# A three-layer kernel on one core: one subtraction moved to GpSimd, layer 2 one slice later, both heads' states in one instruction, contiguous weight slices

## The chip, the cores and the metric

The program runs on one core of one Trainium2 chip. Its engines are TensorE (PE in the profile; its weight loads have a row of their own, PEld), VectorE (DVE), ScalarE (ACT), GpSimd (POOL) and SyncE (SP, which issues DMAs). Each engine works off its own list of instructions in order and waits on semaphores for the others. The metric is the device time of one execution in microseconds (us), the median of several; lower is better.

## The reference

Three layers follow one another. Only the arithmetic that matters here is kept:

```python
# 1: recurrence over S=768 tokens for B=4, H=8, D=48; state is D x D per batch and head
for t in range(S):
    cur   = einsum('bhd,bhe->bhde', u*k[t], v[t])
    y[t]  = einsum('bhd,bhde->bhe', r[t], state + cur)
    state = w[t][..., None]*state + einsum('bhd,bhe->bhde', k[t], v[t])
x = y as (3072 tokens, 384)
# 2: dense layer, w_in 384 x 2048, w_out 2048 x 384
h = maximum(x @ w_in, 0);  x = (h*h) @ w_out
# 3: 8 experts, top 1, tokens with x @ w_skip <= 0 pass unchanged
e = argmax(x @ w_gate);  g = softmax(x @ w_gate)[e]
out = x + g * (maximum(x @ w1[e], 0) @ w2[e])
```

The inputs may come as 64-bit floats; the kernel reads them as words and makes 32-bit floats of the weights itself.

## The kernel before, in words

**Tiling.** The 3072 tokens are cut into 12 units of 256 tokens (`UT`). Stage A computes layer 1 of a unit, stage B layer 2 with the routing scores as ten more output columns, stage C the experts. A and B run as one pipeline: while B works on unit i, A works on a later unit. Stage C begins when all units are through B.

**Precision.** Each float32 operand of layers 2 and 3 is split into two parts, a rounded one (`h` in the names: `xth`, `wih`, `woh`, `gh`) and the rest (`l`: `xtl`, `wil`, `wol`, `gl`), and three products are added. The rest is always made by subtracting the rounded part from the whole.

**Stage B.** One unit has 16 slices of 128 hidden columns. `b_l1` of a slice is nine matmuls of 256 columns into one of two PSUM banks `ph`. ScalarE makes `g` from it by relu and square (L346, L347) and rounds it to `gh` (L348); VectorE subtracts (L349):

```python
        nc.scalar.copy(gh, g)
        nc.vector.tensor_tensor(gl, g, gh.bitcast(F32), ALU.subtract)
```

`b_l2` of the slice is six matmuls of 394 columns (L357) that add to the two PSUM banks `acc`; the third and the sixth read `gl`. There are two sets of `g`, `gh`, `gl`, used in turn. `route` then copies `acc` out (L369, L370), writes the unit's rows and computes each token's place in the lists of the experts, with small VectorE instructions (L385 to L441) and two indirect DMAs from GpSimd (L446).

**Stage A.** A half unit `H` has two head pairs, and `elem(H)` does its elementwise work: two scans on VectorE (L190, L205), products on GpSimd (L198 and L229 `ru`, L210 `bsc`, L241 `kbd`, L235 `gr`), a scaling on ScalarE (L228). From unit 3 on VectorE transposes `kbd` into `knd` (L216). The tensor work of head pair `P` is `pair_steps(P)` with six steps: `s1p` (L265) and `s1v` (masked copies, L275) make the products within chunks of 64 tokens; `s2p` (L286) makes each chunk's addition to the state in `pu`; `s2v` carries the state from chunk to chunk; `s3p` (L310) applies it; `s3v` splits the result into B's operand. In `s2v` each chunk and each of the two heads of a pair has an instruction of its own, of 48 partitions, on VectorE (L300 for a sequence's first chunk, else L302), and the state is written straight into `vz`, where `s3p` reads it:

```python
                for h in range(2):
                    sl = slice(64 - 64 * h, 112 - 64 * h)
                    u_ps = pu[sl, c * 48:(c + 1) * 48]
```

**Weights of B.** For each of 16 slices `w_load` fetches 128 columns of `w_in` and 128 rows of `w_out` by two DMAs from SP, `w_dec` turns words into float32 on VectorE (L509 to L511, tile `stf`), `w_split` rounds on ScalarE (L518, L521) and subtracts on GpSimd or, where the table `lw` has a 1, on VectorE (8 of 32; L520, L522). `w9_tp` to `w9_f` make the ten score columns. `raw` and `stf` have two buffers each. `consts` fills small tables on VectorE (L473 to L478).

**Order.** Every piece of work is put into one list of events with a time in slices of B: `b_l1` of slice g has the time g + 0.09, `b_l2` of slice g the time g + 1.256, and the pieces of A have times from the tables `PRM` (the first units) and `STP` (all later ones). The list is sorted by time and written out; this sets the order on every engine. Nothing is reordered at run time.

Of the kernel before, what the change touches and what calls it, by code (L numbers as in the profile page):

```python
# [84 lines left out]
def rwkv_moe_kernel(ctx: ExitStack, tc: tile.TileContext, a_in, v_in, ud, w_in, w_out,  # L85
# [170 lines left out]
    def pair_steps(P):  # L256
# [56 lines left out]
        def s3v():  # L313
# [3 lines left out]
            if P < 8 and PRM["ly"][P]:  # L317
                yf = bp.tile([128, 2, DM], F32, tag="x2", name="x2", bufs=1)[:, 0, 0:UT]
                nc.scalar.copy(yf, y)
                nc.scalar.copy(hi, yf)  # L320
                nc.gpsimd.tensor_tensor(lo, yf, hi.bitcast(F32), ALU.subtract)
            else:
                nc.scalar.copy(hi, y)
                nc.vector.tensor_tensor(lo, y, hi.bitcast(F32), ALU.subtract)
# [164 lines left out]
    dec, wot = {}, {}  # L489

    def w_load(j):
        s = slice(j * 128, (j + 1) * 128)
        if w_in.dtype == F32:
# [1 line left out]
            nc.sync.dma_start(f[:, 0].rearrange("p (k n) -> p k n", k=KC),
                              w_in[:, s].rearrange("(k p) f -> p k f", p=128))
            nc.sync.dma_start(f[:, 1], w_out[s])
# [550 lines left out]
```

## Time and profile before

| | us |
|---|---|
| median of 3 runs | 980.1 (976.5 to 981.46) |
| span of the profiled execution, first to last instruction | 978.3 |
| VectorE busy | 690.6 |
| TensorE busy | 832.3 |
| GpSimd busy | 413.5 |
| ScalarE busy | 410.0 |

The profiled execution has no time of its own beside its span; the median of the runs stands 1.8 us above that span. The program has five stretches. From 0 to 94 us the first unit of A runs and the first weights are decoded. From 94 to 159 B's first unit runs beside the rest of the weights. From 159 to 641 A and B run together, one unit after another. At 641 a branch on the range of the decays ends the pipeline of A, and B's last unit runs beside the loading of expert weights. From 690 to 978 the experts run. TensorE's busy time is modelled for pipelined matmuls, so the waits of PEld show its stalls best.

### The profile page before, as it was taken

To read this page: it belongs to the slowest core of one execution; us is meant where nothing else is said; L and a number is where in the kernel's file an instruction comes from. 1 tells how busy PE (TensorE), PEld (TensorE's weight loads), DVE (VectorE), ACT (ScalarE), POOL (GpSimd) and SP (SyncE) were. 2 spreads that over 40 slices of the span, in tenths; PEclk is the share of its full clock that TensorE was granted. 3 is DMA by queue.
4 is the path that set the end of the run, shared out by engine and by line. 5 is a ranking of instruction groups with operands and counts; after the bars stand their busy time and mean duration, and the time that the engine had idled before them with its cause. 6 is when DMAs were issued, how large, how long until landed. Compare 5 with 4: busy or idle time off the path is not lost. (4 is left out here: it accounts for less than half of the span.)

```text
span 978.3 us, 17865 instructions
## 1 busy us (share of the span) xinstructions
PE 832.3 (85%) x6528; PEld 772.1 (79%) x6528; DVE 690.6 (71%) x1605; ACT 410.0 (42%) x1020; POOL 413.5 (42%) x409
## 2 busy tenths in 40 slices
PE   2666899999899999899999899989899779787844
PEld 2555799989788888788888788989899779776743
DVE  7997977788888888888888888535633266256631
ACT  1233556545454545454545454457222123123410
POOL 7754635443434343434343434002822256254540
PEclk9999799999999999999999999989999899898877
DMA  8435212231313131313131311055621155153510
GB/s 199 142 127 173 98 44 77 65 80 41 84 37 86 38 90 30 88 33 88 37 99 21 93 27 51 9 167 176 194 66 33 45 173 171 41 180 119 195 32 6
DMA packets 75625, 86.93 MB, mean 89 GB/s; under 512 B 32020, under 2 KB 68008, under 8 KB 75456
## 3 DMA queue, kind: packets, MB, share of 16 engines
q1 hardware_dynamic: 68080, 72.53, 26.2%
q0 software_dynamic: 4736, 11.18, 3.5%
q10 hardware_dynamic: 2640, 1.23, 0.6%
q8 instruction: 74, 1.21, 0.5%
q14 instruction: 95, 0.78, 0.3%
HBM read 68.44 MB, written 15.16 MB: 85 GB/s over the span
## 5 line engine op out<-in xcount | busy, mean ns | idle before, releaser
L342 PE MATMUL ph<-xt,wih 128*128 128x256 f32 x1152 | 226.9, 293 | 3.4 <-PEq L709 3.4
L342 PEld LDWEIGHTS ph<-xt,wih 128*128 128x128 f32 x1152 | 185.0, 192 | 6.7 <-issue 3.7
L342 PE MATMUL ph<-xt,wil 128*128 128x256 f32 x576 | 164.1, 285 | 0.0
L357 PE MATMUL acc<-woh,gl 128*128 128x394 f32 x384 | 136.7, 356 | 29.3 <-DVE gl L349 29.3
L349 DVE TENSOR_TENSOR gl<-g,gh 128x256 fp32r<-128x256 f32 x192 | 98.3, 512 | 78.4 <-ACT gh L348 77.4
L346 ACT ACTIVATE g<-ph 128x256 f32<-128x256 f32 x192 | 73.9, 385 | 183.1 <-PE ph L342 171.3
L357 PE MATMUL acc<-woh,gh 128*128 128x394 f32 x384 | 134.0, 349 | 0.6 <-ACT gh L348 0.6
L357 PE MATMUL acc<-wol,gh 128*128 128x394 f32 x384 | 131.6, 343 | 0.0
L342 PEld LDWEIGHTS ph<-xt,wil 128*128 128x128 f32 x576 | 110.8, 192 | 0.0
L357 PEld LDWEIGHTS acc<-woh,gl 128*128 128x128 f32 x384 | 72.8, 189 | 44.1 <-DVE gl L349 43.6
L229 POOL TENSOR_TENSOR ru<-ain,fsc 112x512 f32<-112x512 f32 x23 | 28.2, 1228 | 180.3 <-ACT ain L228 180.2
L816 DVE SCALAR_TENSOR_TENSOR gl<-ph,gh 128x256 fp32r<-128x256 f32 x80 | 33.6, 422 | 89.0 <-ACT gh L815 88.8
L302 DVE SCALAR_TENSOR_TENSOR vz<-vz,wsw,pu 48x48 f32<-48x48 f32 x320 | 84.3, 263 | 10.3
L275 DVE COPY_PREDICATED gr<-cis,pat 64x256 f32<-64x256 int32 x192 | 85.1, 443 | 8.9 <-PE pat L265 4.6
L815 ACT ACTIVATE gh<-ph 128x256 fp32r<-128x256 f32 x80 | 30.7, 384 | 135.3 <-PE ph L812 135.3
L347 ACT ACTIVATE g<-g 128x256 f32<-128x256 f32 x192 | 80.2, 418 | 6.1
L348 ACT CAST gh<-g 128x256 fp32r<-128x256 f32 x192 | 77.9, 406 | 6.1
L357 PEld LDWEIGHTS acc<-woh,gh 128*128 128x128 f32 x384 | 73.4, 191 | 1.9 <-ACT gh L348 1.2
L357 PEld LDWEIGHTS acc<-wol,gh 128*128 128x128 f32 x384 | 73.4, 191 | 0.0
L772 POOL DMA_INDIRECT out<-yo,lsb x22 | 22.0, 1001 | 113.4 <-DVE yo L771 70.4
L265 PE MATMUL pat<-ru,kbd 112*128 112x128 f32 x384 | 56.5, 295 | 15.4 <-POOL kbd L241 14.5
L265 PEld LDWEIGHTS pat<-ru,kbd 112*128 112x128 f32 x384 | 53.9, 209 | 15.6 <-POOL kbd L241 14.5
(187 smaller groups left out, 1799.3 us busy)
## 6 DMA issues: line engine op xcount, KB each, us to landing
raw<-in_w SPq DMA_DIRECT2D x64, 384.0 KB, 4.1
ain<-in_a_in SPq DMA_DIRECT2D x23, 675.9 KB, 5.2
raw<-in_w_in SPq DMA_DIRECT2D x16, 384.0 KB, 3.9
raw<-in_w_out SPq DMA_DIRECT2D x16, 384.0 KB, 4.5
vz<-in_v_in SPq DMA_DIRECT2D x44, 128.0 KB, 5.2
x2d<-x SPq DMA_DIRECT2D x12, 384.0 KB, 2.5
out<-x SPq DMA_DIRECT2D x12, 384.0 KB, 3.1
xt<-yt SPq DMA_DIRECT2D x72, 32.0 KB, 2.0
```

The source lines that it names most:

```text
L229: nc.gpsimd.tensor_tensor(st["ru"][:, :, :, 1, :], r, st["f"][:, :, :, 1:65], ALU.mult)
L265: nc.tensor.matmul(pat[:, c], kb[0:112, qq, c, :], ru[:, qq, c], start=True, stop=True)
L275: nc.vector.copy_predicated(gr[sl, qq, :, h, :], msk[sl].unsqueeze(1).to_broadcast([64, 4, CH]), pat[sl, :, m, :])
L302: nc.vector.scalar_tensor_tensor(zn, hv[H][sl, qq, c, h, 0:48], wsw[sl, q, b, cg:cg + 1], u_ps, ALU.mult, ALU.add)
L342: nc.tensor.matmul(h[:, 0:UT], w[:, kc, j * 128:(j + 1) * 128], x[:, kc, :], start=(n == 0), stop=(n == 3 * KC - 1))
L346: nc.scalar.activation(g, h[:, 0:UT], AF.Relu)
L347: nc.scalar.activation(g, g, AF.Square)
L348: nc.scalar.copy(gh, g)
L349: nc.vector.tensor_tensor(gl, g, gh.bitcast(F32), ALU.subtract)
L357: nc.tensor.matmul(acc[t][:, 0:OW], a[:, s], w[:, j, :], start=(j == 0 and n == 0), stop=(j == NJ - 1 and n == 2))
L815: nc.scalar.activation(hhs[f % 2], h[:, 0:UT], AF.Relu)
L816: nc.vector.scalar_tensor_tensor(hls[f % 2], h[:, 0:UT], 0.0, hhs[f % 2].bitcast(F32), ALU.max, ALU.subtract)
```

## The change

- **gl on GpSimd.** In `b_l1` the subtraction that makes `gl` is issued on GpSimd instead of VectorE. `gh` and `gl` get three buffers (`NPB`) that slices take in turn; `g` keeps two.
- **Layer 2 later.** `b_l2` of slice g has the time g + 2.256 instead of g + 1.256, except at the ends of the last two units; `route` of units 0 to 9 is one slice later too.
- **States.** `s2v` makes one instruction of 112 partitions for a chunk of both heads, into new tiles `zt` and `zcs`. A new step `s2c` copies the states from there into `vz` on ScalarE: two copies for a pair, four for the second pair of a half unit unless it ends a sequence.
- **Weights.** The host lays `w_in` and `w_out` out as one array `wio`, so that a slice is one contiguous DMA. All 32 subtractions of `w_split` are on GpSimd.
- **First steps.** `consts` moves from time -16.5 to 9. The small copies `o_w` and the scaling `o_us` have times of their own; in steady state `o_w` is 0.9 slices later and `o_us` 0.9 slices earlier. The pool of the decode buffers closes at time 7 instead of 27.3. Some tiles live in other pools.

```diff
 STP = {
-    "b": [0.09, 1.256],
+    "b": [0.09, 2.256],
 PRM = {
-    "c": -16.511,
+    "c": 9,
...
+        def o_us():
+            r, k, w = hin[H]
+            if H >= 4 or PRM["lu"][H]:
+                for q in range(2):
+                    nc.scalar.activation(r[:, q], r[:, q], AF.Copy, scale=uds[:, q0 + q:q0 + q + 1])
...
         def s2v():
+            zt, zc = zts[P % 2], zcs[:, q]
             for c in range(4):
                 cg = 4 * th + c
                 if cg == 11:
                     continue
-                for h in range(2):
-                    sl = slice(64 - 64 * h, 112 - 64 * h)
-                    u_ps = pu[sl, c * 48:(c + 1) * 48]
-                    zn = (hv[H][sl, qq, c + 1] if c < 3 else vzs[(H + 2) % 3][sl, qq, 0])[:, h, 0:48]
...
+                u_ps = pu[0:112, c * 48:(c + 1) * 48]
+                zn = zt[:, c] if c < 3 else zc
+                if cg == 0:
+                    nc.vector.tensor_copy(zn, u_ps)
+                else:
+                    nc.vector.scalar_tensor_tensor(zn, zt[:, c - 1] if c else zc, wsw[:, q, b, cg:cg + 1], u_ps,
+                                                   ALU.mult, ALU.add)
+
+        def s2c():
+            zt = zts[P % 2]
+            for h in range(2):
+                sl = slice(64 - 64 * h, 112 - 64 * h)
+                nc.scalar.copy(hv[H][sl, qq, 1:4, h, 0:48], zt[sl])
+                if qq and th < 2:
+                    nc.scalar.copy(vzs[(H + 2) % 3][sl, :, 0, h, 0:48], zcs[sl, q - 1:q + 1])
...
-        g, gh, gl = pgs[j % 2]
+        g = pgg[j % 2]
+        gh, gl = pgs[(NJ * i + j) % NPB]
...
-        nc.vector.tensor_tensor(gl, g, gh.bitcast(F32), ALU.subtract)
+        nc.gpsimd.tensor_tensor(gl, g, gh.bitcast(F32), ALU.subtract)
...
-        sv = w_in.bitcast(I32)[:, 2 * j * 128:2 * (j + 1) * 128].rearrange("(k p) f -> p k f", p=128)
-        nc.sync.dma_start(raw[:, 0].rearrange("p (k n) -> p k n", k=KC), sv)
-        nc.sync.dma_start(raw[:, 1], w_out.bitcast(I32)[s])
+        nc.sync.dma_start(raw.rearrange("p a b -> p (a b)"), wio.bitcast(I32)[j])
...
-        lo = [nc.vector if PRM["lw"][2 * j + n] else nc.gpsimd for n in range(2)]
-        lo[0].tensor_tensor(wil[:, :, s], fi, wih[:, :, s].bitcast(F32), ALU.subtract)
+        nc.gpsimd.tensor_tensor(wil[:, :, s], fi, wih[:, :, s].bitcast(F32), ALU.subtract)
...
-            atv(16 * (i + 1) + (STP["r"][n] if n or i < NU - 2 else 0.01), f)
+            atv(16 * (i + 1) + (1 + STP["r"][n] if i < NU - 2 else STP["r"][n] if n else 0.01), f)
...
-        atv(g + (0.9 if g == TB - 1 else STP["b"][1]), lambda g=g: b_l2(g // 16, g % 16))
+        atv(g + {TB - 2: 1.5, TB - 1: 0.9, TEND - 2: 1.9, TEND - 1: 1.256}.get(g, STP["b"][1]),
+            lambda g=g: b_l2(g // 16, g % 16))
...
-    run_to(8 * 2 * TDU - LEAD - 3 + 0.3)
+    run_to(7)
```

On TensorE, in unit 7, this stands behind `b_l1` of its slice 2. Before, `gh_116` and `gl_117` are the buffers of odd slices, so these are the six matmuls of slice 1:

```order
L342 MATMUL ph_69<-xt_108,wil 128x256
L357 MATMUL acc_71<-woh,gh_116 128x394
L357 MATMUL acc_71<-wol,gh_116 128x394
L357 MATMUL acc_71<-woh,gl_117 128x394
L357 MATMUL acc_72<-woh,gh_116 128x394
L357 MATMUL acc_72<-wol,gh_116 128x394
L357 MATMUL acc_72<-woh,gl_117 128x394
L286 MATMUL pu<-vz_121,knd_1746 48x48 x8
```

Now, at the same place, the buffers go by the slice's number in the program modulo 3 (114, 116, 118 for `gh`); `gh_116` has been written by slice 0:

```order
L356 MATMUL ph_69<-xt_108,wil 128x256
L372 MATMUL acc_71<-woh,gh_116 128x394
L372 MATMUL acc_71<-wol,gh_116 128x394
L372 MATMUL acc_71<-woh,gl_117 128x394
L372 MATMUL acc_72<-woh,gh_116 128x394
L372 MATMUL acc_72<-wol,gh_116 128x394
L372 MATMUL acc_72<-woh,gl_117 128x394
L298 MATMUL pu<-vz_123,knd_975 48x48 x8
```

The work of A stands where it stood; the matmuls of layer 2 are those of a slice earlier.

On GpSimd, for the second half unit of a unit in steady state, this stood before, with nothing of B in it:

```order
L235 TENSOR_TENSOR gr_123<-ru,wst 48x8x64 x2
L198 TENSOR_TENSOR ru<-ain,fsc 112x8x64
L210 TENSOR_TENSOR bsc<-bsc,gi 112x8x64
L241 TENSOR_TENSOR kbd_119<-ain,bsc 48x8x64 x2
L235 TENSOR_TENSOR gr_124<-ru,wst 48x8x64 x2
L229 TENSOR_TENSOR ru<-ain,fsc 112x8x64
```

Now the same pieces have the subtractions among them:

```order
L244 TENSOR_TENSOR gr_125<-ru,wst 48x8x64 x2
L203 TENSOR_TENSOR ru<-ain,fsc 112x8x64
L364 TENSOR_TENSOR gl_115<-g_112,gh_114 128x256
L364 TENSOR_TENSOR gl_117<-g_113,gh_116 128x256
L364 TENSOR_TENSOR gl_119<-g_112,gh_118 128x256
L215 TENSOR_TENSOR bsc<-bsc,gi 112x8x64
L250 TENSOR_TENSOR kbd_121<-ain,bsc 48x8x64 x2
L244 TENSOR_TENSOR gr_126<-ru,wst 48x8x64 x2
L364 TENSOR_TENSOR gl_115<-g_113,gh_114 128x256
L364 TENSOR_TENSOR gl_117<-g_112,gh_116 128x256
L238 TENSOR_TENSOR ru<-ain,fsc 112x8x64
```

Five instructions of A (one `bsc`, two `kbd`, two `gr`) stand in one piece between two subtractions; elsewhere there are fewer.

On VectorE, at the start of the program, this stood before, behind the work of the first half unit:

```order
L224 SCALAR_TENSOR_TENSOR ru<-ain,uds,fsc 112x4x64 x2
L473 MEMSET cum 128x8
L474 CAST tribf<-cfs 128x128
L475 CAST onebf<-cfs 128x128
L476 COPY pay<-cis 128x24
L477 MEMSET lsb 128x384
L478 COPY lsb<-cis 128x192
L190 SCALAR_TENSOR_TENSOR fsc<-ain,rst 112x520
L275 COPY_PREDICATED gr_123<-cis,pat 64x4x64 x4
```

Now:

```order
L235 SCALAR_TENSOR_TENSOR ru<-ain,uds,fsc 112x4x64 x2
L192 SCALAR_TENSOR_TENSOR fsc<-ain,rst 112x520
L287 COPY_PREDICATED gr_125<-cis,pat 64x4x64 x4
L210 SCALAR_TENSOR_TENSOR bsc<-ain,rst 112x521
L211 RECIPROCAL gi<-fsc 112x8
```

The six instructions of `consts` are gone from there; they stand behind slice 8 of the first unit.

## Rows read from the trace of the kernel before

**Rows 1.** The page's first part: busy us, share of the span, instructions.
```profile
PE 832.3 (85%) x6528; PEld 772.1 (79%) x6528; DVE 690.6 (71%) x1605; ACT 410.0 (42%) x1020; POOL 413.5 (42%) x409
```

**Rows 2.** Windows: stretch, length, busy us of PE, PEld, DVE, ACT, POOL, clock, DMA.
```profile
0.00:94.00 94.00, 49.04 (x298) 42.30 (x299) 78.35 (x120) 26.51 (x72) 56.09 (x72) 1.00 0.56 159
94.00:159.00 65.00, 60.72 (x491) 56.88 (x491) 52.72 (x103) 36.02 (x97) 34.58 (x36) 0.92 0.29 82
...
205.30:595.00 389.70, 362.32 (x3217) 331.64 (x3216) 339.01 (x904) 196.08 (x504) 164.67 (x177) 1.00 0.24 59
...
641.00:690.00 49.00, 47.78 (x317) 45.91 (x318) 26.44 (x84) 31.84 (x72) 12.03 (x9) 0.94 0.53 170
690.00:978.00 288.00, 225.72 (x1439) 214.96 (x1437) 128.57 (x210) 71.74 (x156) 117.01 (x88) 0.89 0.34 107
```

**Rows 3.** Timeline of ACT: start, length; one unit's result copied out, eight units apart.
```profile
205.34 0.86 ACT L370 COPY x<-acc 128x384 f32<-128x384 f32 x2 [2.31 <-DVE lg L369]
...
595.00 0.86 ACT L370 COPY x<-acc 128x384 f32<-128x384 f32 x2 [2.10 <-DVE lg L369]
```

**Rows 4.** Waits of PEld, 0 to 640 and 205.3 to 595: us in total, times, longest.
```profile
PEld acc L357 <- DVE gl L349: 42.6, 43, 1.9
...
PEld acc L357 <- DVE gl L349: 39.2, 38, 1.9
```

**Rows 5.** Timeline, four engines, 399 to 406 us; idle time before it in brackets.
```profile
399.31 2.87 POOL L241 TENSOR_TENSOR kbd<-ain,bsc 48x512 f32<-48x512 f32 x2
...
400.99 1.22 DVE L387 TENSOR_TENSOR ohf<-ohf,cfs 128x16 f32<-128x16 f32 x1
...
404.60 0.42 DVE L349 TENSOR_TENSOR gl<-g,gh 128x256 fp32r<-128x256 f32 x1
...
405.07 0.19 PEld L357 LDWEIGHTS acc<-woh,gl 128*128 128x128 f32 x1 [1.90 <-DVE gl L349]
```

**Rows 6.** Groups by form, 205.3 to 595: count, busy us, mean ns, idle before.
```profile
L349 DVE TENSOR_TENSOR gl<-g,gh 128x256 fp32r<-128x256 f32 x128 | 67.4, 527 | 31.9 <-ACT gh L348 31.2
L302 DVE SCALAR_TENSOR_TENSOR vz<-vz,wsw,pu 48x48 f32<-48x48 f32 x216 | 56.9, 263 | 7.0
...
L387 DVE TENSOR_TENSOR ohf<-ohf,cfs 128x16 f32<-128x16 f32 x8 | 9.7, 1216 | 0.3
...
L300 DVE COPY vz<-pu 48x48 f32<-48x48 f32 x22 | 4.5, 206 | 0.7
...
L241 POOL TENSOR_TENSOR kbd<-ain,bsc 48x512 f32<-48x512 f32 x33 | 41.7, 1264 | 2.4
...
L210 POOL TENSOR_TENSOR bsc<-bsc,gi 112x512 f32<-112x512 f32 x16 | 16.6, 1038 | 0.7
...
L228 ACT ACTIVATE ain<-ain,uds 112x256 f32<-112x256 f32 x32 | 14.5, 502 | 0.0
```

**Rows 7.** Groups of DVE by form, 641 to 690.
```profile
L387 DVE TENSOR_TENSOR ohf<-ohf,cfs 128x16 f32<-128x16 f32 x2 | 0.4, 176 | 0.1
```

**Rows 8.** Timeline of DVE and PE, 13 to 18 us.
```profile
13.36 1.18 DVE L474 CAST tribf<-cfs 128x128 bf16<-128x128 f32 x1
...
16.72 1.23 DVE L190 TENSOR_TENSOR_SCAN fsc<-ain,rst 112x520 f32<-112x520 f32 x1
...
14.51 2.08 PE L265 MATMUL pat<-ru,kbd 112*128 112x128 f32 x8 [14.51 <-POOL kbd L241]
```

**Rows 9.** Groups of DVE, then POOL, by form, 0 to 126 us.
```profile
L509 DVE TENSOR_SCALAR stf<-raw 128x768 int32<-128x768 int32 x16 | 15.2, 953 | 2.2 <-DMA raw<-in_w_out 2.2
...
L302 DVE SCALAR_TENSOR_TENSOR vz<-vz,wsw,pu 48x48 f32<-48x48 f32 x40 | 10.5, 263 | 1.3
...
L522 DVE TENSOR_TENSOR wol<-stf,woh 128x384 fp32r<-128x384 f32 x5 | 4.2, 837 | 0.0
...
L520 DVE TENSOR_TENSOR wil<-stf,wih 128x384 fp32r<-128x384 f32 x3 | 1.7, 556 | 0.3 <-ACT wih L518 0.2
...
L520 POOL TENSOR_TENSOR wil<-stf,wih 128x384 fp32r<-128x384 f32 x13 | 15.7, 1209 | 20.7 <-ACT wih L518 20.7
```

More of the change, by code (lines that the diff above doesn't have):

```diff
@@ L144, in rwkv_moe_kernel @@
     dp = sD.enter_context(tc.tile_pool(name="dp", bufs=1, side="left"))
-    pgs = [[bp.tile([128, UT], d, name=f"{n}{i}") for n, d in (("g", F32), ("gh", F32R), ("gl", F32R))]
-           for i in range(2)]
+    pgg = [bp.tile([128, UT], F32, name=f"g{i}") for i in range(2)]
+    pgs = [[bp.tile([128, UT], F32R, name=f"{n}{i}") for n in ("gh", "gl")] for i in range(NPB)]
     kbd = [ap.tile([128, 2, 4, 128], F32, name=f"kbd{i}") for i in range(2)]
@@ L152, in rwkv_moe_kernel @@
     yt4 = ap.tile([128, 2, UT], F32R, name="yt4")
+    zts = [ap.tile([112, 3, 48], F32, name=f"zt{i}") for i in range(2)]
+    zcs = ap.tile([112, 4, 48], F32, name="zcs")
     rst = ap.tile([112, 521], F32, name="rst")
@@ L190, in o_scan, with o_w @@
             nc.vector.tensor_tensor_scan(ff, w[:, 0:520], rst[:, 0:520], 0.0, ALU.mult, ALU.add)
+        def o_w():
+            f = st["f"]
             nc.gpsimd.tensor_copy(wst[:, q0:q0 + 2, b, 1 + 4 * th:5 + 4 * th], f[:, :, :, 64])
@@ L226, in o_u @@
                 return
-            for q in range(2):
-                nc.scalar.activation(r[:, q], r[:, q], AF.Copy, scale=uds[:, q0 + q:q0 + q + 1])
             nc.gpsimd.tensor_tensor(st["ru"][:, :, :, 1, :], r, st["f"][:, :, :, 1:65], ALU.mult)
@@ L248, in o_g @@
                                  accum_out=gmin[:, H:H + 1])
-        ops = list(enumerate([o_scan, o_r, o_back, o_rec, o_k, o_g, o_u, o_rz]))
+        gap = 0.0005 if H < 4 else 0.9
+        ops = [(n, 0, f) for n, f in enumerate([o_scan, o_r, o_back, o_rec, o_k, o_g, o_u, o_rz])]
+        ops += [(0, gap, o_w), (6, -gap, o_us)]
         if H // 2 >= TDU:
-            ops += [(8 + 2 * h + a, lambda h=h, a=a: o_t(h, a)) for h in range(2) for a in range(2)]
+            ops += [(8 + 2 * h + a, 0, lambda h=h, a=a: o_t(h, a)) for h in range(2) for a in range(2)]
         return ops
@@ L316, in s3v @@
             hi, lo = (xt[:, 0, q], xt[:, 1, q]) if q < 3 else (yt4[:, 0], yt4[:, 1])
[L317 to L324, printed above, removed]
+            nc.scalar.copy(hi, y)
+            nc.vector.tensor_tensor(lo, y, hi.bitcast(F32), ALU.subtract)
             if q == 3:
@@ L329, in s3v @@
                                           yt4[64 * h + 16 * z:64 * h + 16 * z + 16].bitcast(F32))
-        return s1p, s1v, s2p, s2v, s3p, s3v
+        return s1p, s1v, s2p, s2v, s2c, s3p, s3v
     gts = {}
+    x2p = [None]
     def b_l1(i, j):
@@ L470, in rwkv_moe_kernel @@
         nc.gpsimd.memset(t, 0.0)
+    nc.vector.memset(pu[0:112, 0:192], 0.0)
     def consts():
@@ L491, in w_load @@
     def w_load(j):
[L492 to L493 removed]
+        if wio.dtype == F32:
             dec[j] = f = dp.tile([128, 2, DM], F32, tag="stf", name="stf", bufs=2)
[L495 to L497 removed]
+            nc.sync.dma_start(f.rearrange("p a b -> p (a b)"), wio[j])
             return
         dec[j] = raw = dp.tile([128, 2, 2 * DM], I32, tag="raw", name="raw", bufs=2)
[L500 to L502 removed]
+        nc.sync.dma_start(raw.rearrange("p a b -> p (a b)"), wio.bitcast(I32)[j])
     def w_dec(j):
[L505 removed]
+        if wio.dtype == F32:
             return
@@ L557, in rwkv_moe_kernel @@
     for H in range(NHF):
-        for m, (k, f) in enumerate(elems[H]):
-            atv(PRM["e"][H][m] if H < 4 else 8 * H - LEAD - 8 + STP["e"][H % 2][k], f)
+        for k, d, f in elems[H]:
+            atv((PRM["e"][H][k] if H < 4 else 8 * H - LEAD - 8 + STP["e"][H % 2][k]) + d, f)
         if H >= 2:
@@ L565, in rwkv_moe_kernel @@
             if P < 8:
[L566 removed]
+                atv(PRM["p"][P][n - (n > 3)] + (0.2 if n == 4 else 0), f)
             else:
@@ L595, in rwkv_moe_kernel @@
         nc.gpsimd.memset(t, 0.0)
+    x2p[0] = kp
     GA = 4 * (NPG - 1) - LEAD + 3
@@ L790, in rwkv_moe_kernel @@
     xls += [cq.tile([128, KC, UT], F32R, name=f"cxl{i}") for i in range(2, 4)]
-    hhs, hls = [x[1] for x in pgs], [x[2] for x in pgs]
+    hhs, hls = [x[0] for x in pgs], [x[1] for x in pgs]
     hrs = cq.tile([128, FE], F32, name="hr")
```

24 lines of the change are left out of this document (10 added, 14 removed), and 6 rows, old and new, of tables (PRM, STP).

## The prediction

> **What bounds the kernel now.** I read the page's totals first, then busy time by stretch, then who made TensorE's weight loads wait, then a few microseconds of the timeline. In the totals no engine is full [rows 1]; the limit shows only by stretch. From 205.3 to 595 us eight units of 16 slices run exactly alike, with VectorE busy for 339.0 of 389.7 us and GpSimd for 164.7 at full TensorE clock [rows 2]. A unit takes (595.00 - 205.34) / 8 = 48.7 us [rows 3]. There TensorE's loads wait 39.2 us for one thing, `gl` from VectorE, in 38 pieces of about 1 us, the longest 1.9 [rows 4]. That is 4.9 us a unit; without it the same TensorE work takes 48.7 - 4.9 = 43.8 us. The timeline shows how a wait arises [rows 5]: VectorE is inside the routing's small instructions, `gl` starts only at 404.60, and the load that reads it starts at 405.07 after 1.90 us of idling. `gl` itself is short; it is late because it stands in a queue that is 87% busy, while layer 2 wants it one slice after it can be made.
>
> Ahead of that, from 0 to 94, VectorE is busy 78.4 of 94 us and TensorE 49.0 [rows 2]: decoding weights sets the pace. From 690 on the experts run, which the change leaves alone.
>
> **The steady units.** The change takes two loads off VectorE. The `gl` row is 67.4 us over eight units, 8.4 a unit. The state rows are 56.9 + 4.5 = 61.4 us; the duration goes with the free size, which stays 48 columns, so one instruction for two heads halves them, 3.8 a unit [rows 6]. VectorE: 42.4 - 8.4 - 3.8 = 30.2 us a unit.
>
> GpSimd gets 16 subtractions of 256 columns a unit, a shape that it never runs before. The nearest rows are its two-input products of 512 columns, 1.04 us (`bsc`) to 1.26 us (`kbd`) [rows 6]. The lower bound is half of the one, 0.52, were there no fixed part; the upper is the whole of the other, 1.26. I take 0.7, half of either plus some fixed part. GpSimd: 20.6 + 16 x 0.7 = 31.8 us a unit, with bounds 28.9 and 40.8. ScalarE gets about 11 small state copies a unit; not above its `L228` row's 0.50 us each [rows 6], so 24.5 + 5.5 = 30.0 us at most. All three stay below TensorE's 43.8 us, even at the upper bounds, so TensorE becomes the bound.
>
> Demand is not lateness, however. The order gives `gl` one more slice, 43.8 / 16 = 2.7 us, which is more than the longest old wait, 1.9. Against it, GpSimd works in order, and a subtraction now stands behind whatever of A is in front. The worst place is the piece of five (one `bsc`, two `kbd`, two `gr`): some 1.0 + 2 x 1.26 + 2 x 1.05 = 5.7 us, against about two slices that pass between `gh` and its use. I reckon with 1 us of waiting left per unit there, with bounds 0 and 2.5. What queues behind a late `gl` is ScalarE's relu two slices on, since `g` has two buffers; that has another slice of slack. The indirect DMAs of the routing wait on GpSimd for VectorE's addresses, and `gl` is behind them now, but VectorE no longer follows the slices and should have them ready; I cost that at nothing, and at up to 3 us a unit if the cover fails.
>
> In the whole stretch to 640 the old waits are 42.6 us [rows 4]. With ten such units and 1 us left in each: -42.6 + 10 = -33 us (bounds -43 and -18).
>
> **A rule against the move.** A small VectorE product of 16 columns, `L387`, takes 1.22 us in the steady stretch [rows 6] and 0.18 when GpSimd idles [rows 7]; in the timeline it falls into a running `kbd` [rows 5]. So the engines hold each other up. The Trainium skill (SBUF — State Buffer, "Who interferes with whom") says that a VectorE instruction with two SBUF inputs and a GpSimd instruction that reads SBUF exclude each other, the loser blocking until the other is done; these rows agree. What follows here: GpSimd goes from 42% to 73% of a unit, so such VectorE products meet it more often, by 73/42. The one known excess, 1.04 us a unit, becomes 1.8; other small products of the routing may do the same. VectorE has 13 us of room a unit, and `gl`, the most frequent two-input instruction, leaves it. I add nothing; the rival below takes the case in which the lock falls on GpSimd.
>
> **The first 126 us.** VectorE loses there 4.2 + 1.7 = 5.9 us of weight subtractions, five `gl` at 0.53 (2.6), half of the states (40 rows of 10.5 us and eight plain copies at 0.21, half of 12.2 is 6.1), and `consts`, from 13.36 to 16.72, 3.4 [rows 6, 8, 9]: together 18 us. Not all of it is on the path. Of `consts` at most 1.3 us is: the masked copies behind them wait for the `pat` matmuls, which end at 16.6 [rows 8]. The subtractions go to GpSimd at 1.21 us each instead of 0.56 to 0.84 [rows 9], 8 x 1.21 + 5 x 0.7 = 13 us on an engine with 56.1 of 94 us busy [rows 2], and `stf` is free only after them. A state now passes through ScalarE before TensorE uses it. The single DMA of a slice can give no more than the 2.2 us that VectorE waited for `raw` [rows 9], and a faster VectorE will wait for `raw` more often. I take 10 us of the 18; the bounds are 2, as if GpSimd took nearly all back, and 18. `consts` and the clearing of `knd` fall into the first unit later, where VectorE and GpSimd have room for them: nothing.
>
> **The ends.** B's last unit waits hardly for `gl`; it keeps its length [rows 2], with half a microsecond less at its end, since two slices of layer 2 stand between the last `b_l1` and the last `gl`. The experts' 288 us stay.
>
> **The sum.** On the profiled execution: 978.3 - 33 - 10 - 0.5 = 934.8 us. The median of the runs stands 1.8 above that span, so 936.6; I predict 936.
>
> **The rivals.**
> - *gl is late in bursts.* GpSimd's demand fits, but its pieces of 3 to 6 us make several `gl` a unit late, and 2.5 us a unit remain; the first stretch gives 6 us. 978.3 - (42.6 - 25) - 6 + 1.8 = 956. For it: one queue now holds A's long products and B's most urgent instruction, as VectorE's did. Against it: the second slice of slack. Chance 20%.
> - *The wait moves to the state.* `s3p` now waits for ScalarE's copies, which stand behind a slice's relu, square and rounding. At 1.2 us for each of four pairs a unit that is 4.8, all that was won; only the first 10 us remain: 970. Against it: four VectorE instructions in place of eight save 1 us per pair on the same path. Chance 5%.
> - *No change.* GpSimd takes back in the first stretch what VectorE gives, and a wait on the order of the old one remains: 976 to 984. Chance 4%.
> - *Slower: GpSimd becomes the bound through the lock.* If each subtraction waits for a VectorE scan or masked copy, GpSimd's demand passes the old 48.7 us from (48.7 - 20.6) / 16 = 1.75 us per `gl`. At 2.0 us it is 52.6, so 3.9 more in each of ten units, with the first 10 us still won: 978.3 + 39 - 10 + 1.8 = 1009. Against it: GpSimd's rows of twice the width stay at 1.04 to 1.26 us beside a VectorE that is 87% busy. Chance 5%.
>
> **How the numbers follow.** My forecast has 66%; its own range is 920 to 948, from the bounds of the waits left (0 to 2.5) and of the first stretch. With the bursts the range is 918 to 958; above it lie the last three cases, and below it the case that both terms come out at their best, some 5%. A measurement of this kernel can't tell less than about 0.5% from no change, here 5 us. Faster by more: the forecast, the bursts and the state, 91%. Within: 4%. Slower: 5%.
>
> **What would show it.** Right: units of 44 to 45 us between their copied results; PEld's waits for `gl` below 15 us in all, now on GpSimd; `gl` rows at 0.6 to 0.8 us; VectorE busy some 540 us and GpSimd some 560; B's first slice at about 86 us instead of 94; the experts as long as before. Wrong: `gl` above 1.3 us, waits of TensorE for `vz` from ScalarE, GpSimd idle before `lst` with `gl` behind it, or a first slice that is not earlier.

## The result, and the profile after

The changed kernel takes 951.1 us (median of 4 runs, 949.4 to 952.4) against 979.9 for the kernel before on the same chip: a ratio of 0.9715, 95% interval 0.9678 to 0.9752. That is 2.9% faster, and 15 us slower than the 936 predicted. The profiled execution has a span of 948.8 us, 29.5 less than before.

The page's first part after (engine, busy us, share, instructions), against [rows 1]:

```profile
PE 825.0 (87%) x6528; PEld 771.7 (81%) x6528; DVE 560.6 (59%) x1230; ACT 440.3 (46%) x1148; POOL 571.3 (60%) x609
```

The windows of the changed kernel (stretch, length, busy us of PE, PEld, DVE, ACT, POOL, clock, DMA), against [rows 2]:

```profile
0.00:94.00 94.00, 45.08 (x299) 38.42 (x300) 73.61 (x92) 28.30 (x83) 64.52 (x73) 0.77 0.53 156
94.00:126.00 32.00, 25.37 (x195) 23.59 (x195) 31.27 (x35) 19.90 (x59) 27.59 (x25) 0.87 0.37 120
209.30:568.10 358.80, 356.93 (x3218) 334.70 (x3217) 246.02 (x655) 217.52 (x593) 257.30 (x304) 1.00 0.26 64
```

The copies of a unit's result on ScalarE, eight units apart, against [rows 3]:

```profile
209.32 1.01 ACT L385 COPY x<-acc 128x384 f32<-128x384 f32 x2 [1.26 <-DVE lg L384]
...
568.10 1.02 ACT L385 COPY x<-acc 128x384 f32<-128x384 f32 x2 [1.12 <-DVE lg L384]
```

What is left of the weight loads' wait for `gl`, 0 to 640 and 209.3 to 568.1 us, against [rows 4]; then the group of `gl` on GpSimd and three VectorE groups in the second stretch (count, busy us, mean ns, idle before), against [rows 6]:

```profile
PEld acc L372 <- POOL gl L364: 3.2, 12, 0.6
...
PEld acc L372 <- POOL gl L364: 1.6, 8, 0.3
```

```profile
L364 POOL TENSOR_TENSOR gl<-g,gh 128x256 fp32r<-128x256 f32 x128 | 97.2, 760 | 82.2 <-ACT gh L363 57.5 <-issue 11.3 <-POOL gl L364 6.2
...
L210 DVE TENSOR_TENSOR_SCAN bsc<-ain,rst 112x521 f32<-112x521 f32 x16 | 26.6, 1666 | 0.0
...
L313 DVE SCALAR_TENSOR_TENSOR zt<-zt,wsw,pu 112x48 f32<-112x48 f32 x64 | 17.0, 265 | 2.3
...
L402 DVE TENSOR_TENSOR ohf<-ohf,cfs 128x16 f32<-128x16 f32 x8 | 1.4, 174 | 0.3
```

The reader is to see a steady stretch that has become TensorE's: it is busy 356.9 of 358.8 us, and a unit takes (568.10 - 209.32) / 8 = 44.8 us instead of 48.7. The waits for `gl` fell from 39.2 to 1.6 us. GpSimd itself waits 57.5 us for `gh`; TensorE loses 1.6 us by it in these eight units.

To see where the 29.5 us lie, I take the start of ScalarE's relu of a slice as a mark, since it follows TensorE directly. The mark of the second unit's first slice, before and after:

```profile
156.55 0.38 ACT L346 ACTIVATE g<-ph 128x256 f32<-128x256 f32 x1 [1.57 <-PE ph L342]
```

```profile
158.75 0.39 ACT L361 ACTIVATE g<-ph 128x256 f32<-128x256 f32 x1 [1.57 <-PE ph L356]
```

| stretch, by that mark | before | after | difference |
|---|---|---|---|
| start to slice 8 of the first unit | 133.0 | 132.2 | -0.8 |
| slice 8 to the second unit | 23.5 | 26.5 | +3.0 |
| second unit | 45.2 | 45.9 | +0.7 |
| eight steady units | 389.9 | 358.9 | -30.9 |
| last two units | 86.0 | 83.5 | -2.5 |
| rest, with the experts | 300.7 | 301.7 | +1.0 |

The differences are those of the unrounded marks. The gain is in the steady units, with a little in the last two. The first unit, from which 10 us were to come, ends 2.2 us later.

### The profile page after: what moved, and what is told of

It reads as the page before. It is cut to its first block, busy times and chain, and to the rows that moved or that the text cites. A ratio compares the mean times of both kernels' runs of the same rounds, so it can differ in the third digit from the quotient of the medians.

```text
span 948.8 us, 17902 instructions
## 1 busy us (share of the span) xinstructions
PE 825.0 (87%) x6528; PEld 771.7 (81%) x6528; DVE 560.6 (59%) x1230; ACT 440.3 (46%) x1148; POOL 571.3 (60%) x609
## 5 line engine op out<-in xcount | busy, mean ns | idle before, releaser
L364 POOL TENSOR_TENSOR gl<-g,gh 128x256 fp32r<-128x256 f32 x192 | 150.2, 784 | 141.4 <-ACT gh L363 89.1
L372 PE MATMUL acc<-woh,gl 128*128 128x394 f32 x384 | 132.7, 346 | 1.6 <-POOL gl L364 1.6
L372 PE MATMUL acc<-woh,gh 128*128 128x394 f32 x384 | 133.0, 346 | 0.0
L287 DVE COPY_PREDICATED gr<-cis,pat 64x256 f32<-64x256 int32 x192 | 85.4, 445 | 32.2 <-PE pat L277 28.0
L221 DVE STREAM_TRANSPOSE knd<-kbd 32x256 f32<-32x256 f32 x144 | 62.4, 433 | 3.6 <-POOL kbd L250 1.1
L250 POOL TENSOR_TENSOR kbd<-ain,bsc 48x512 f32<-48x512 f32 x48 | 59.2, 1233 | 3.2 <-DVE bsc L215 0.7
```

What stands on the lines that cost most here:

```text
L221: nc.vector.transpose(kn[64 * h + 32 * b2:64 * h + 32 * b2 + 32, :, :, 64 * h + 32 * a:64 * h + 32 * a + 32], kb[64 * h + 32 * a:64 * h + ...
L250: eng("lk", H).tensor_tensor(st["kb"][sl, :, :, 64 * h:64 * h + 64], k[sl], st["rc"][sl], ALU.mult)
L287: nc.vector.copy_predicated(gr[sl, qq, :, h, :], msk[sl].unsqueeze(1).to_broadcast([64, 4, CH]), pat[sl, :, m, :])
L364: nc.gpsimd.tensor_tensor(gl, g, gh.bitcast(F32), ALU.subtract)
L372: nc.tensor.matmul(acc[t][:, 0:OW], a[:, s], w[:, j, :], start=(j == 0 and n == 0), stop=(j == NJ - 1 and n == 2))
```

## The experiments

The two kernels and the twelve runs in one table: start of B's first matmul, the marks of slice 8 and of the second unit, mean of the eight steady units (us of one profiled execution each), then the median of the timed runs and the ratio to the kernel before, which was timed again beside each group of runs on their chip (medians of 978.1 to 980.0 us).

| kernel | first | slice 8 | 2nd unit | steady | median | ratio [95%] |
|---|---|---|---|---|---|---|
| before | 93.9 | 133.0 | 156.6 | 48.7 | 979.9 | |
| after | 93.6 | 132.2 | 158.8 | 44.9 | 951.1 | 0.9715 [0.9678, 0.9752] |
| e4_gl_vector | 95.0 | 134.9 | 160.0 | 50.1 | 992.5 | 1.0119 [1.0080, 1.0157] |
| e5_one_slice | 92.7 | 132.3 | 160.5 | 51.1 | 1021.8 | 1.0436 [1.0401, 1.0470] |
| e8_old_states | 93.0 | 132.1 | 157.5 | 45.7 | 954.7 | 0.9756 [0.9728, 0.9784] |
| e1_old_split | 92.6 | 131.9 | 158.3 | 44.9 | 949.7 | 0.9695 [0.9666, 0.9724] |
| e2_all_split_vector | 90.1 | 129.8 | 156.2 | 44.9 | 947.4 | 0.9679 [0.9652, 0.9706] |
| e3_copies_later | 91.3 | 129.7 | 156.2 | 44.9 | 948.1 | 0.9675 [0.9646, 0.9704] |
| e6_vz_earlier | 91.7 | 129.5 | 156.0 | 44.9 | 946.9 | 0.9681 [0.9654, 0.9708] |
| e7_products_later | 93.2 | 131.3 | 155.3 | 44.9 | 948.4 | 0.9697 [0.9670, 0.9724] |
| c1_all_four | 87.5 | 125.2 | 149.3 | 45.0 | 942.8 | 0.9638 [0.9606, 0.9670] |
| c2_without_split | 88.8 | 127.8 | 151.8 | 45.0 | 941.6 | 0.9634 [0.9603, 0.9665] |
| c3_raw_earlier | 85.0 | 124.3 | 148.3 | 44.9 | 939.1 | 0.9599 [0.9570, 0.9627] |
| b1_before_vz_earlier | 93.2 | 131.3 | 154.8 | 48.3 | 975.3 | 0.9976 [0.9951, 1.0001] |

The stretch behind the last mark alone varies from 297 to 304 us between these executions, though none of the edits touches it. So a single edit of the first stretch, worth 2 to 4 us, is read from the marks, one execution each; by time, its interval overlaps that of the changed kernel. Differences of marks below are taken before rounding.

### The steady units: is it the engine, the later slice, or both?

**gl back on VectorE, layer 2 still two slices later.**

```diff
-        nc.gpsimd.tensor_tensor(gl, g, gh.bitcast(F32), ALU.subtract)
+        nc.vector.tensor_tensor(gl, g, gh.bitcast(F32), ALU.subtract)
```

> The changed kernel with gl back on VectorE; layer 2 stays two slices behind layer 1. Theory C (the later slice cures the waits, whatever the engine): VectorE does some 39 us of a unit, but a late gl still comes in time; units of 45 to 46 us, 950 to 962. Theory D (a queue that is nearly full stays late): units of 47 to 48.5 us with 2 to 4 us of waits for gl each, 970 to 985.

Measured: 992.5 us, slower than the kernel before. The waits of this kernel between 210 and 570 us (engine, line, what it waited for: us, times, longest):

```profile
PEld py L329 <- ACT vz L320: 12.9, 12, 1.8
PEld pu L298 <- DVE knd L221: 10.7, 7, 1.5
...
PEld acc L372 <- DVE gl L364: 1.7, 6, 0.3
...
DVE gl L364 <- ACT gh L363: 70.5, 43, 2.8
```

Both theories fall. The later slice does cure the lateness of `gl`: 1.7 us of waits are left. But VectorE now stands still 70.5 of 360 us in front of `gl` until `gh` is there (29.9 us in the same stretch of the kernel before), and TensorE waits for the state and for `knd` instead, which VectorE makes behind it. The rows of `gl` themselves take 66.1 us. That the standing still, and not this length, makes A's instructions late is argued and not shown: no run has the one without the other.

**gl on GpSimd, layer 2 one slice behind as before.**

```diff
-    "b": [0.09, 2.256],
+    "b": [0.09, 1.256],
-            atv(16 * (i + 1) + (1 + STP["r"][n] if i < NU - 2 else STP["r"][n] if n else 0.01), f)
+            atv(16 * (i + 1) + (STP["r"][n] if i < NU - 2 else STP["r"][n] if n else 0.01), f)
```

> The changed kernel with layer 2 again one slice behind layer 1 (and the routing one slice sooner, as before); gl stays on GpSimd. Theory F (it was the engine: VectorE no longer stops for gh): units of 45 to 46 us, 951 to 962. Theory G (both parts are needed, since GpSimd's pieces of 2.5 to 5 us now stand ahead of gl with one slice of slack): waits of 2 to 4 us a unit for gl from GpSimd come back, units of 47 to 48.5, 970 to 983.

Measured: 1021.8 us, outside both ranges on theory G's side. The wait for `gl` between 210 and 570 us:

```profile
PEld acc L372 <- POOL gl L364: 32.1, 22, 3.7
```

One place of it, in GpSimd's and TensorE's timelines (start, length, idle before it in brackets):

```profile
372.29 1.05 POOL L215 TENSOR_TENSOR bsc<-bsc,gi 112x512 f32<-112x512 f32 x1
373.42 2.42 POOL L250 TENSOR_TENSOR kbd<-ain,bsc 48x512 f32<-48x512 f32 x2
375.91 2.14 POOL L244 TENSOR_TENSOR gr<-ru,wst 48x512 f32<-48x512 f32 x2
378.13 1.41 POOL L364 TENSOR_TENSOR gl<-g,gh 128x256 fp32r<-128x256 f32 x2
```

```profile
375.15 0.34 PE L372 MATMUL acc<-wol,gh 128*128 128x394 f32 x1
378.91 0.69 PE L372 MATMUL acc<-woh,gl 128*128 128x394 f32 x1 [3.41 <-POOL gl L364]
379.40 0.53 PE L372 MATMUL acc<-woh,gh 128*128 128x394 f32 x1
```

Two `gl` stand behind a piece of five products that runs from 372.29 to 378.05, and TensorE idles 3.41 us. This is the worst place that the prediction named; with the second slice of slack all waits for `gl` come to 0.2 us a unit, without it to 32.1 us over 360 / 51.1 = 7 units, 4.6 a unit. A unit is 6.2 us longer than the changed kernel's. The waits for `gl` and for `gh` (3.7 us, 0.5 a unit) leave some 1 us of that, and the rows suggest where it lies: behind a wait the matmul of 0.34 us takes 0.53, and the windows show the granted clock between its two levels, 2.4 GHz (1.00) and half of it:

```profile
370.00:375.00 5.00, 5.00 (x49) 4.69 (x48) 2.54 (x10) 3.04 (x9) 3.27 (x4) 1.00 0.00 0
375.00:380.00 5.00, 1.59 (x7) 1.26 (x6) 1.76 (x4) 2.96 (x9) 4.79 (x6) 0.78 0.00 0
380.00:385.00 5.00, 5.00 (x34) 4.31 (x34) 2.69 (x14) 0.76 (x2) 0.68 (x1) 0.54 0.67 172
```

So neither part of the change works alone; each alone is slower than the kernel before, beside the other new parts.

**States of the two heads apart again.** `s2v` is that of the kernel before, which writes `vz` from VectorE, and the copies are dropped:

```diff
         def s2c():
-            zt = zts[P % 2]
...
+            pass
```

> The changed kernel with the states of the two heads again in two VectorE instructions that write vz directly, and no copies on ScalarE. Prediction's reading: VectorE does 3.8 us a unit more, below its limit, so the steady units stay at 44.8 to 45.3; in the first stretch VectorE loses 6 us against the copies that go from ScalarE: 950 to 955. Theory B (the copies cost more there than the halved instructions gave): 945 to 949.

Measured: 954.7 us, in the range of the first reading, though the intervals of the two ratios overlap. The steady unit is 45.7, 0.8 longer than with the new states and beyond the 45.3 expected; TensorE waits there for `knd` and `gl` (8.7 and 6.6 us in 360, against 2.8 and 1.6). The second unit starts 1.2 us sooner, as theory B has it. So by the marks the states in one instruction are worth 6.4 us in the eight steady units and cost 1.2 in the first.

### The first stretch: where did VectorE's 18 us go?

VectorE's busy time from 0 to 126 us fell from 107.73 to 104.88 us, 2.9 instead of 18. The two decoding rows with two inputs in the kernel before, beside [rows 9], then the decoding in the changed kernel and GpSimd's subtractions:

```profile
L510 DVE SCALAR_TENSOR_TENSOR stf<-raw,stf 128x768 int32<-128x768 int32 x16 | 20.2, 1264 | 0.6
L511 DVE SCALAR_TENSOR_TENSOR stf<-raw,stf 128x768 int32<-128x768 int32 x16 | 19.1, 1191 | 0.6
```

```profile
L522 DVE SCALAR_TENSOR_TENSOR stf<-raw,stf 128x768 int32<-128x768 int32 x16 | 24.5, 1529 | 0.6
L521 DVE SCALAR_TENSOR_TENSOR stf<-raw,stf 128x768 int32<-128x768 int32 x16 | 23.6, 1473 | 0.6
L520 DVE TENSOR_SCALAR stf<-raw 128x768 int32<-128x768 int32 x16 | 15.8, 987 | 4.4 <-POOL wol L532 3.2 <-DMA raw<-in_wio 1.2
...
L532 POOL TENSOR_TENSOR wol<-stf,woh 128x384 fp32r<-128x384 f32 x15 | 20.6, 1372 | 0.0
L530 POOL TENSOR_TENSOR wil<-stf,wih 128x384 fp32r<-128x384 f32 x16 | 20.2, 1262 | 14.9 <-ACT wih L529 13.0 <-issue 1.8
```

The 18 us did leave. But the three decoding instructions, unchanged in the code, take 63.9 us where they took 54.5 (20.2, 19.1 and 15.2), and a fifth pair of scans falls into the stretch.

**The split as before (8 of 32 subtractions on VectorE).**

```diff
+    "lw": [0, 0, 0, 0, 0, 0, 1, 0, 0, 1, 0, 0, 0, 1, 0, 0, 1, 1, 0, 0, 0, 0, 0, 0, 0, 0, 0, 1, 0, 1, 1, 0],
...
-        nc.gpsimd.tensor_tensor(wil[:, :, s], fi, wih[:, :, s].bitcast(F32), ALU.subtract)
+        lo = [nc.vector if PRM["lw"][2 * j + n] else nc.gpsimd for n in range(2)]
+        lo[0].tensor_tensor(wil[:, :, s], fi, wih[:, :, s].bitcast(F32), ALU.subtract)
...
-        nc.gpsimd.tensor_tensor(wol[:, j, 0:DM], f[:, 1], woh[:, j, 0:DM].bitcast(F32), ALU.subtract)
+        lo[1].tensor_tensor(wol[:, j, 0:DM], f[:, 1], woh[:, j, 0:DM].bitcast(F32), ALU.subtract)
```

> The changed kernel with one part undone: 8 of the 32 subtractions that split the weights go back to VectorE, by the old table. Theory A (GpSimd takes back what VectorE gave in the first stretch: the decoding instructions of two inputs run slower beside its subtractions, and VectorE waits for the last wol): the rows of the two-input decoding fall from 1.53 and 1.47 us to about 1.3 and 1.2, the 3.2 us wait for wol goes, yt of the first unit comes 2 to 4 us sooner than 79.4, the first unit ends near 160 instead of 163.7, and the time is 945 to 949. Theory B (the new state copies on ScalarE hold up the casts of the weights): nothing of that moves, 950 to 953. The steady units stay at 44.8 us by either.

Measured, by its decoding rows:

```profile
L523 DVE SCALAR_TENSOR_TENSOR stf<-raw,stf 128x768 int32<-128x768 int32 x16 | 22.9, 1432 | 0.6
L522 DVE SCALAR_TENSOR_TENSOR stf<-raw,stf 128x768 int32<-128x768 int32 x16 | 20.6, 1291 | 0.6
L521 DVE TENSOR_SCALAR stf<-raw 128x768 int32<-128x768 int32 x16 | 14.6, 910 | 1.3 <-DMA raw<-in_wio 1.0 <-DVE wil L532 0.2
```

The two rows fall to 1.43 and 1.29 us, the wait for `wol` goes, `yt` comes 1.2 us sooner, at 78.18, but the second unit starts only 0.4 sooner; 949.7 us. VectorE has the eight subtractions again (6.6 us) and waits 4.0 us for ScalarE's casts in front of them. Theory A is right on the rows and too large in the sum. The decoding takes 58.1 us here, so 5.8 of the 9.4 us that it grew by go with the eight subtractions. With the same split the kernel before took 54.5; where the other 3.6 us come from no run shows.

**All 32 subtractions on VectorE** (`"lw": [1] * 32`).

> The changed kernel with all 32 subtractions of the weight split on VectorE, so that GpSimd has none in the first stretch. Theory A: the two-input decoding rows fall to 1.1 us or below (16 x 0.8 us back), while 32 subtractions at about 0.6 us (19 us) come on: VectorE's busy time in the first 126 us grows by some 6 us and the time stays within 948 to 955. If the slow rows had nothing to do with GpSimd they stay near 1.5, VectorE has 19 us more to do, and the time is 960 to 970. Theory B: also 960 to 970, since nothing is taken from ScalarE.

Measured: 947.4 us, just below the range of theory A. VectorE's rows of this kernel, and the window from 0 to 126 of the changed kernel and of this one:

```profile
L522 DVE SCALAR_TENSOR_TENSOR stf<-raw,stf 128x768 int32<-128x768 int32 x16 | 17.3, 1079 | 0.6
L523 DVE SCALAR_TENSOR_TENSOR stf<-raw,stf 128x768 int32<-128x768 int32 x16 | 17.2, 1073 | 0.6
L534 DVE TENSOR_TENSOR wol<-stf,woh 128x384 fp32r<-128x384 f32 x16 | 12.5, 778 | 0.0
...
L521 DVE TENSOR_SCALAR stf<-raw 128x768 int32<-128x768 int32 x16 | 10.5, 656 | 1.4 <-DMA raw<-in_wio 1.2
L532 DVE TENSOR_TENSOR wil<-stf,wih 128x384 fp32r<-128x384 f32 x16 | 10.3, 644 | 2.8 <-ACT wih L530 2.7
```

```profile
0.00:126.00 126.00, 70.44 (x492) 62.02 (x493) 104.88 (x127) 48.20 (x141) 92.11 (x98) 0.80 0.49 147
```

```profile
0.00:126.00 126.00, 76.17 (x510) 67.63 (x511) 104.61 (x159) 49.96 (x146) 52.43 (x70) 0.69 0.50 148
```

VectorE does 32 subtractions more, 22.8 us, and is busy as long as without any of them: 104.6 against 104.9 us. The decoding alone falls from 63.9 to 45.0 us, now that GpSimd has 40.8 us less to do beside it. The Trainium skill (SBUF — State Buffer, "Who interferes with whom") says that a VectorE instruction with two inputs in SBUF and a GpSimd instruction that reads SBUF exclude each other; the two decoding rows with two inputs agree, 1.50 us on average against 1.08. The one with a single input (0.99 against 0.66) slows down as well; why is not shown. The Trainium skill (Perfetto Trace Analysis, "Optimizing Scalar/DVE Operations") warns that moving work from VectorE to GpSimd might not help for this reason; in this stretch it did not, by these rows.

**ScalarE's copies of the state later.**

```diff
-                atv(PRM["p"][P][n - (n > 3)] + (0.2 if n == 4 else 0), f)
+                atv(PRM["p"][P][n - (n > 3)] + (0.447 if n == 4 else 0), f)
```

> The changed kernel with the state copies of the first eight head pairs issued a quarter of a slice later on ScalarE, just ahead of the matmuls that read them, so that more casts of weights stand before them. Theory B: ScalarE's wait for the state falls from 21 us to under 12, the casts come sooner, and the time is 945 to 949. Theory A: ScalarE's wait only changes its name, 950 to 953.

Measured: ScalarE's wait for the state, 0 to 94 us, in the changed kernel and in this one:

```profile
ACT vz L320 <- DVE zt L313: 21.1, 4, 5.4
```

```profile
ACT vz L320 <- DVE zt L313: 8.8, 2, 6.3
```

The second unit starts 2.5 us sooner, 948.1 us. So theory B holds beside theory A: copies that wait stand ahead of casts that could run.

**A load of `vz` sooner.** It is issued from ScalarE's queue at 82.93, behind a copy that waits, and lands at 92. TensorE in the changed kernel (start, length, idle before):

```profile
92.26 0.87 PE L298 MATMUL pu<-vz,kn 128*48 128x48 f32 x14 [3.70 <-DMA vz<-in_v_in]
93.06 0.90 PE L536 MATMUL ptk<-cfs,stf 128*128 128x128 f32 x3
93.62 0.78 PE L356 MATMUL ph<-xt,wih 128*128 128x256 f32 x2
```

In the kernel before TensorE waits for this load 0.48 us, and then 2.51 us in front of its `ptk` matmuls (TensorE, with the last decoding instruction of VectorE between):

```profile
89.91 0.88 PE L286 MATMUL pu<-vz,kn 128*48 128x48 f32 x14 [0.48 <-DMA vz<-in_v_in]
...
92.23 1.01 DVE L511 SCALAR_TENSOR_TENSOR stf<-raw,stf 128x768 int32<-128x768 int32 x1
...
93.30 0.90 PE L526 MATMUL ptk<-cfs,stf 128*128 128x128 f32 x3 [2.51 <-DMA vz<-in_v_in]
93.85 0.78 PE L342 MATMUL ph<-xt,wih 128*128 128x256 f32 x2
```

The profile puts the second wait down to a load of `vz` too. But these matmuls read `stf`, not `vz`, and the decoding of `stf` ends at 92.23 + 1.01 = 93.24, 0.06 us before they start: it is a wait for a decoded weight.

```diff
-    "l": [-10.475, -5.82, -1.923, 0.573],
+    "l": [-10.475, -5.82, -4.9, 0.573],
```

> The changed kernel with the load of v for half unit 2 (vz) issued three slices sooner, ahead of the copies of xt. Theory H (a gate common to both kernels swallowed VectorE's gain: TensorE waits 3.7 us for this load from 88.6 to 92.3, and the first slice follows): the wait goes, the first slice starts at 89 to 91 instead of 93.6, the second unit starts 2.5 to 4 us sooner than 158.8, 947 to 949. Theory A or B alone (VectorE's decode or the casts set the pace there too): the wait turns into one for a cast or a decode, first slice at 92.5 to 94, 950 to 952.

Measured: the wait goes, and one for a decoded weight takes its place:

```profile
91.14 0.90 PE L536 MATMUL ptk<-cfs,stf 128*128 128x128 f32 x3 [2.31 <-DVE stf L522]
```

The first slice starts at 91.7, between the two ranges, and the second unit 2.8 us sooner; 946.9 us. The decoding itself ends 1.3 us sooner (91.09 instead of 92.39), since VectorE no longer waits 1.17 us for `raw` there.

**The same in the kernel before.**

> The kernel before with its load of vz for half unit 2 issued three slices sooner and nothing else. Theory H (a gate common to both kernels): TensorE's wait of 2.5 us for it goes, the first slice starts at 91 to 92.5 instead of 93.9, 976 to 978.5. Without such a gate: 979 to 981.

Measured: the 0.48 us go, and TensorE waits for the decoded weight as before:

```profile
92.60 0.90 PE L526 MATMUL ptk<-cfs,stf 128*128 128x128 f32 x3 [2.47 <-DVE stf L511]
```

The first slice starts 0.7 us sooner, as the decoding does, and the second unit 1.7. The ratio to the kernel before is 0.9976 [0.9951, 1.0001], no change that can be told; its eight steady units too are 3.2 us shorter, which the edit doesn't touch. So theory H is wrong in its common gate: the load held up the changed kernel, and in the kernel before the decoding did. In the changed kernel the load came last by little: `ptk` starts at 93.06, its weight was decoded at 92.39. That e6 gave 1.9 us at the first slice and not 0.7 is the `raw` that came sooner with it.

**The products that read the state later.**

```diff
-        ... [1.965, 1.965, 2.491, 2.965, 3.413, 3.965], [7.963, 7.963, 8.489,
-        8.963, 9.411, 9.963], [9.001, 9.001, 9.527, 10.001, 10.449, 11.001]],
+        ... [1.965, 1.965, 2.491, 2.965, 4.113, 4.665], [7.963, 7.963, 8.489,
+        8.963, 10.111, 10.663], [9.001, 9.001, 9.527, 10.001, 11.149, 11.701]],
```

> The changed kernel with the products that read the states (s3p and what follows) of head pairs 5 to 7 placed 0.7 slice later. Theory J (in the second half of the first unit TensorE waits for the state's copies on ScalarE, some 2 to 3 us of the 3 that this half is longer than before): the waits of py for vz from ScalarE between 126 and 157 go from 2.4 us to under 0.5, the second unit starts 1.5 to 3 us sooner than 158.8, 948 to 950. If that half is longer for the work of GpSimd there: no change, 951.

Measured: this wait of the changed kernel, 126 to 158 us, is gone:

```profile
PEld py L329 <- ACT vz L320: 1.4, 3, 0.6
```

Slice 8 to the second unit takes 24.0 us instead of 26.5 (23.5 before), and the second unit starts 3.4 us sooner; 948.4 us. The wait is 1.4 of the 2.5 us; the rest is not accounted for. This is the rival of the prediction in which the wait moves to the state, true in the first unit alone: there the table left 0.45 of a slice between state and product, and the copies came between.

**All four edits (e2, e3, e6, e7), the last three, and the four with two weight loads sooner.** The third moves two loads of `raw` ahead of the copies of `xt` on SyncE's queue, and one decode ahead of pair 4's masked copies:

```diff
-        ... [-0.927, -0.927, -0.078, ... [-0.2, -0.2, 0.649, ...
+        ... [-2.9, -1.3, -0.078, ... [-2.85, -0.2, 0.649, ...
```

> The changed kernel with four edits together: all weight subtractions on VectorE, state copies a quarter slice later, vz loaded earlier, products of pairs 5 to 7 later. If the four take away separate waits of the first stretch they add up: the second unit starts 9 to 12 us sooner than 158.8, 937 to 941. If the first three take away one and the same wait before the first slice: 5 to 7 us sooner, 943 to 946. The steady units stay at 44.8.

> The same without the moved subtractions (they stay on GpSimd). Theory A: the subtractions' place is worth 2 to 3 us beside the others, 940 to 944; if GpSimd's part is covered by the others, the same as with all four.

> The four edits, and the loads of weight slices 10 and 11 ahead of the copies of xt on SyncE's queue, with slice 10 decoded before the masked copies of pair 4. If VectorE's wait of 5.9 us for pat, with the next weights not yet there, is what is left: VectorE decodes in it, the slices from the third on come 2 to 4 us sooner, and the time is 2 to 4 us below that of the four. If the casts or ScalarE set the pace by then: no difference.

Measured: with all four the second unit starts 9.5 us sooner than in the changed kernel; the four alone gave 2.5, 2.5, 2.8 and 3.4, together 11.2. They mostly add up, as separate waits. The time, 942.8 us, lies between the two ranges. Without the moved subtractions the mark is 2.6 us later, but the time is the same (941.6): their worth beside the others is not settled by time. With the two loads sooner the first slice starts 2.5 us sooner still. The third and later ones were expected to gain 2 to 4 us and gain 0.1 to 1.0, the second unit 0.9. The median of 939.1 us is the lowest here, 4.0% below the kernel before [3.7, 4.3] and by disjoint intervals below the changed kernel.

## Why the prediction was right or wrong

**Direction and mechanism: right.** TensorE became the bound of the steady units, and the later slice and the other engine are both needed (e4, e5). The median of 951.1 us lies above the forecast's own range, 920 to 948, and within the wider one with the bursts, 918 to 958. That is luck: the wider range was there for late `gl`, which did not come, and another term filled it. The 948 was not the end of the bounds either: with -18 and -2 the sum comes to 978.3 - 18 - 2 - 0.5 + 1.8 = 959.6.

**The steady units: right, in size partly by luck.** Predicted 44.8 us a unit, measured 44.8; VectorE 30.2 a unit, measured 246.0 / 8 = 30.8; GpSimd 31.8, measured 32.2; ScalarE at most 30.0, measured 27.2; `gl` 0.7 us, measured 0.76. One us of waiting left a unit was too much, it is 0.2. So the work without these waits takes 44.6 us a unit and not 43.8: two misses of 0.8 us cancel. The 43.8 took all waiting of the weight loads off the unit, 39.2 us in eight; in the kernel before the matmuls themselves waited less for `gl`:

```profile
PE acc L357 <- DVE gl L349: 26.9, 38, 1.6
```

The eight units gained 30.9 us, between the two, so the waits of the loads overstate what TensorE loses by them. From the second unit to the last but one the marks give -31.9 us for the -33 of the sum.

**The rule against the move.** The small product that was slowed to 1.22 us takes 0.17 now: it no longer falls beside GpSimd's long ones (at 434.57, with GpSimd idle from 433.30 to 436.43). It was not the only one (the `ohf` products at L386 and L395 took 0.69 and 0.88 us before). After the change others are slow, the backward scan above all (1.67 us; 1.24 where `gl` is on VectorE, in e4), 0.9 us a unit, then `cum` (L441, 0.92 instead of 0.16) and `t` (L418, 0.58 instead of 0.17), all with two inputs, and `gs` (L426, 0.75 instead of 0.17) with one; the engine has room for it. Adding nothing was right here.

**"The first 126 us": this step failed.** Of 18 us I took 10, with bounds 2 and 18, and the second unit starts 2.2 us later instead. That is 12 of the 14 us by which the sum missed the span of 948.8. The runs put three things in its place. First, the price of the move: I weighed the lock for the steady stretch and charged GpSimd's time, but not the decoding that runs beside it and slows by 9.4 us (5.8 of them go with the eight moved subtractions, e1); e2 shows that the subtractions on GpSimd save VectorE nothing. Second, what was left had to pass gates that no row of the sum had, the load of `vz` (e6) and close behind it the decoding, which itself waits for `raw`: the first slice starts at 93.6 after 93.9. Third, the state's way over ScalarE, which I named without a price: copies ahead of casts (e3) and, in the first unit, products waiting for copies (e7). Taken away together they give 9.5 us (c1), and the second unit then starts 7.3 us before that of the old kernel, 8.2 with the two loads (c3).

**The ends: right within a microsecond.** -0.5 predicted, +0.1 measured.

**Rivals.** `gl` late in bursts does not occur (1.6 us in eight units), though with one slice it would (e5). The wait for the state occurs in the first unit (e7), hardly in the steady ones (1.8 us in eight). Slower through the lock does not occur. Of the signs of error named beforehand two came: TensorE's waits for `vz` from ScalarE, and a first slice that is not earlier (0.2 us).

What stays open: why VectorE waits 70.5 us for `gh` in e4 and 29.9 in the kernel before, and what the moved subtractions are worth in time beside the other edits. The single load of a slice, the move of `consts`, the third buffer of `gh` and `gl` and the new places of `o_w` and `o_us` were not undone by themselves; no run shows what each is worth.

## What to carry to other kernels

An instruction that waits for a distant producer takes from an in-order queue its wait beside its length (70.5 and 66.1 us in e4): give it an engine that can afford both, and enough slack for the longest piece of work in that engine's queue; either alone made this kernel slower. Before work goes from VectorE to GpSimd in a stretch where both are busy, count the two-input instructions that will run beside it: they can give back all that was saved. In a lead-in, freed time on one engine is worth only what comes through the next gate; list who waits just before the first result, in both kernels, and price those waits first.

## What was not expected of the hardware

The subtraction of 128 x 256 on GpSimd takes 0.76 us in the steady units and 1.03 in the first 126 us, on VectorE 0.53 [rows 6] and 0.55; GpSimd's takes longer in the stretch in which VectorE decodes.

TensorE's clock is 1.00 in the whole steady stretch of the changed kernel, and in e5 falls to 0.54 of full speed for the five microseconds behind an idle time of 3.41 us, so that a wait costs more than its length. In the first stretch the recorded clock is no guide: between 50 and 94 us it reads 0.50 to 0.54 after the change and 1.00 before, yet eight `pat` matmuls last 2.05 us in both (from 84.74 and 85.61 us; from 130.44 before, where it also reads 1.00, they last 1.05), and e4, with 1.00 from 0 to 94, starts its first slice later than any other kernel.
